# Four products g side by side, TensorE's part of the attention at fewer places, and six buffers for the last x2

## The chip, the cores and the metric

The kernel runs on 1 core of one Trainium2 chip. The metric is the device time of one execution in microseconds (us). TensorE is called PE here, VectorE DVE, ScalarE ACT, GpSimd POOL and SyncE, which issues all DMAs of this kernel, SP.

## The reference, cut to what matters

Three parts follow each other: an attention with 32 memory slots per head over 8 batches of 576 tokens (8 heads of 64), a first feed-forward block (maximum of three products, then an output product) and a second one (a gated product, then an output product).

```python
def _attn_ref(q, k, v, phi):
    a = exp(phi - max(phi, axis=2)); a = a / (sum(a, axis=2) + 1e-09)
    k_m = einsum('bhsm,bhsd->bhmd', a, k)
    v_m = einsum('bhsm,bhsd->bhmd', a, v)
    scores = (1 / sqrt(64)) * q @ k_m.T
    attn = exp(scores - max(scores)); attn = attn / (sum(attn) + 1e-09)
    return attn @ v_m

# x: attention output as 4608 tokens x 512
h = maximum(maximum(x @ w1, x @ w2), x @ w3)        # 4608 x 768
x2 = h @ moe_w_out                                  # 4608 x 512
gate = 1 / (1 + exp(-(x2 @ w_gate)))                # 4608 x 1536
out = gate * (x2 @ w_val) @ moe2_w_out              # 4608 x 512
```

The weights are float64; the kernel turns their bits into float32 itself. Every product is made of three: each operand is held as a high and a low part in fp32r, and high x low, low x high and high x high are summed (PASSES).

## The kernel before, in words

**Passes.** The first feed-forward block runs in four passes `p` (0 to 3) of two batches, "pairs" in the words of the change. A pass has 24 steps of a first stage (`s` from 0 to 23) and 16 steps of a second one (24 to 39). In the first stage `s = 4 j + u`, where `j` (0 to 5) is a block of 128 of the 768 hidden columns.

**g.** `v_m` times the three weights, for one block `j` and one quarter `hp` of the heads (`g_step`, L383): three products over all 128 rows of the array, 384 columns wide, into one PSUM bank. ACT copies out the high part, DVE subtracts and gives the low part. Each step of the first stage makes one g of the block after its own.

**h.** Attention weights times g, for block `j` and half the tokens of the two batches (`h_part`, L402): 36 products per step, each on 64 rows, two batches beside each other in the array. Two steps fill six banks (three weights, two batches). ACT copies the first pair of banks out (`h_copy`), DVE takes the maximum with the second and the third (`h_max`), ACT and POOL split the result into high and low (`h_keep`).

**x2.** A step of the second stage makes `h @ moe_w_out` for 288 tokens and 128 columns (`x2_step`, L441): 18 products over all 128 rows. DVE or ACT copies the bank into a tile x2 (`x2_keep`, L456), and a DMA stores it. Tile x2 has two buffers.

**Attention.** The attention of the next pass (four sets of heads `n`) is woven into the pass in ten stages a0 to a9 and a split (`stages`, L212 to L334), one stage in a step. PE works in a2 (5 transposes), a3 (40 small products on `kv`, in tiles of 32 columns), a4 (2 transposes) and a5 (8 products with `q`, in tiles of 64 columns). Set `n` begins at step `a_at + 8 n`, with `a_at` 5 in pass 0 and 2 later, so that three sets or so stand in the first stage. `load_ahead` (L618) loads `phi`, `kv` and `q` of the next set when stages 1, 3 and 5 of a set are reached.

**Weights.** In pass 0 each weight tile wx is loaded raw, turned into float32 by two ACT and three DVE instructions on tile ca (`w_f32`, L126), split by ACT and POOL one step later, and stored; later passes load the stored tile. `w_next` is called once a step for this. The weights of the second feed-forward block are converted in the passes 1 to 3 (`b_next`, 13, 13 and 22 times), spread over steps 1 to 37 of passes 1 and 2 and over the first stage of pass 3.

**Order.** In the passes each engine works through its instructions in the order in which the program gives them, and so does SP with its DMAs; within a step this order is: what is due first (`h_max` of the third weight, copies of x2), PE's attention, g, h or x2, `h_copy`, the weight splits, the copies of g, those of the attention, `h_keep`, the conversions, `h_max` of the second weight, loads, stores. There are 8 PSUM banks. In the prologue, in the second stage of pass 3 and after it a planner places the instructions by its own estimates. After the passes comes the second feed-forward block (tiles px, pz, pv, po), for which the PSUM banks are handed over (L774 to L777).

```python
            g = None
            if s < NS:
                j, u = divmod(s, 4)
                if j + 1 < J:
                    g = g_step(p, j + 1, u)
                    next(g)
                h_part(p, j, u // 2, u % 2 == 0)
```

Of the kernel before, what the change touches and what calls it, by code (L numbers as in the profile page):

```python
# [18 lines left out]
def attn_moe_kernel(  # L19
# [148 lines left out]
    def load_phi(n):  # L168
        st = A[n] = {"kv": [], "q": []}
        if n in (2, 3):  # L170
            st["phi"] = early(S)
        else:
            st["phi"] = att.tile([128, S], F32, tag="phi", name="phi", bufs=2)
        for b in range(2):
            m, pr = source(n, b)
            dma(st["phi"][64 * b:64 * b + 64], phiT[m, 64 * pr:64 * pr + 64])

    def load_kv(n):
        for c in (0, 2):
            if n < 4:  # L180
                t = early_tile()[:, :1024]
            else:
                t = att.tile([128, 1024], F32, tag="kv", name="kv", bufs=3)
            t = t.rearrange("p (c x) -> p c x", c=2)
            for b in range(2):
                m, pr = source(n, b)
                dma(t[:, :, 256 * b:256 * b + 256],
                    kvm[m, c:c + 2, :, 256 * pr:256 * pr + 256].rearrange("c s x -> s c x"))
            A[n]["kv"] += [t[:, 0], t[:, 1]]
        if n < 4:  # L190
            t = early(512)
        else:
            t = att.tile([128, 512], F32, tag="kvt", name="kvt", bufs=1)
        for b in range(2):
            m, pr = source(n, b)
            dma(t[:64, 256 * b:256 * b + 256], kvt[m, :, 256 * pr:256 * pr + 256])
        A[n]["kv"].append(t)

    def load_q(n, e):
        if (n, e) in ((0, 0), (0, 1)):  # L200
            t = early(S)
        else:
            t = att.tile([128, S], F32, tag="q", name="q", bufs=3)
        m, pr = source(n, e)
        dma(t, qT[m, pr])
        A[n]["q"].append(t)
# [112 lines left out]
    def a9(n):  # L319
        st = A[n]  # L320
        yield
        stg = st["stg"] = att.tile([128, S], F32, tag="stg", name="stg", bufs=4)
        vec.transpose(out=stg, in_=st["s"].rearrange("p a m -> p (a m)"))

    AT = {}
# [128 lines left out]
        return ps  # L454

    def x2_keep(p, u, d, ps):  # L456
        t = low.tile([128, U], F32, tag="x2", name="x2", bufs=2)
        copy(vec if u % 2 == 0 or p == NP - 1 else act, t, ps[:, :U])
        t0 = p * 2 * S + u * U
        return lambda: dma(x2s[:, d, t0:t0 + U], t)  # L460

    def run(*gens):
        gens = list(gens)
        while gens:
            gens = [x for x in gens if next(x, 1) is None]
# [151 lines left out]

    def load_ahead(k, n):  # L618

        if n + 1 < NBG:  # L620
            if k == 1:
                load_phi(n + 1)
            elif k == 3:
                load_kv(n + 1)
            elif k == 5:
                load_q(n + 1, 0)
                load_q(n + 1, 1)
# [5 lines left out]
    for hp in range(4):  # L633
        w_step()
        run(g_step(0, 0, hp))
    bplan = [(j + h * NJ, n) for j in range(NJ) for h in range(2) for n in range(4)]


# [9 lines left out]
    for p in range(NP):  # L648
        last = p == NP - 1
        side, loads, convs = {}, {}, {}  # L650

        def at(pos, fn, *a, where=None):
            where = side if where is None else where
            where.setdefault(min(int(pos), NS + NX - 1), []).append((fn, a))

        if last:
            att.release()
            br = tc.alloc_tile_pool(name="br", bufs=1, side="right", reuse_waits="tile")
            at(NS, x_load, 0)
            at(NS, tw_load, 0)  # L660
            at(NS + 1, x_sums, 0, 0)
            at(NS + 2, x_sums, 0, 1)
            at(NS + 2, t_make, 0, ORDER[0])
            for n, pr in enumerate(ORDER):
                at(NS + 3 + n * 0.8, x_split, 0, pr, vec if n % 2 else None)
                if n:
                    at(NS + 8 + n * 0.8, t_make, 0, pr)
            at(NS + 14, wo_make, 0)

        def w_next():  # L670
            if plan:
                w_want(*plan.pop(0))
            split, store = w_have()
            if split:
                later["splits"].append(split)
            if store:
                later["stores"].append(store)

        def b_next():
            store = b_have()  # L680
            if store:
                later["stores"].append(store)

        for j in range(2, J):
            for hp in range(4):
                at(4 * (j - 2) + hp, w_next, where=convs)
        if p == 0:
            def wo1_begin():
                plan.extend((-1, n, 0) for n in range(J * DM // PC))
                w_fill()  # L690
            at(4 * (J - 2) - 3, wo1_begin, where=loads)
            for n in range(J * DM // PC):
                at((17, 19, 21, 23, 25, 27, 28, 29)[n], w_next, where=convs)
        if not last:
            def w1_begin(p=p):
                plan.extend((j, hp, p + 1) for j in range(J) for hp in range(4))
                w_fill()
            at(28, w1_begin, where=loads)
            for n in range(8):
                at(30 + n, w_next, where=convs)  # L700
        if p:
            def b_start():
                while len(bq) < 2 and bplan:
                    b_want()
            n_b = 22 if last else 13
            end = NS - 1 if last else NS + NX
            at(0, b_start, where=loads)
            for n in range(n_b):
                at(1 + n * (end - 1) / n_b, b_next, where=convs)
        a_at = 2 if p else 5  # L710
        atts = {}
        if not last:
            if p == 0:
                for n, k in enumerate((1, 3, 5)):
                    at(n, load_ahead, k, 3, where=loads)
            for n in range(4):
                for k in range(len(stages)):
                    atts.setdefault(a_at + 8 * n + k, []).append((k, 4 * p + 4 + n))
                at(max(NS + n, a_at + 8 * n + len(stages)), a_split, 4 * p + 4 + n)
        for s in range(NS + NX):  # L720
            if last and s == NS:
                order["kept"] = queue["in order"] = False
                mid.release()
                b1 = tc.alloc_tile_pool(name="b1", bufs=1, side="right", reuse_waits="tile")
            later = {"first": [], "splits": [], "stores": []}
            hold = []
            take("first")
            gens = [stages[k](n) for k, n in sorted(atts.get(s, ()), reverse=True)]
            for x in gens:
                next(x)  # L730
            g = None
            if s < NS:
                j, u = divmod(s, 4)
                if j + 1 < J:
                    g = g_step(p, j + 1, u)
                    next(g)
                h_part(p, j, u // 2, u % 2 == 0)
            else:
                d, u = divmod(s - NS, 4)
                if not last and 32 <= s < 36:  # L740
                    g = g_step(p + 1, 0, s - 32)
                    next(g)
                ps = x2_step(p, u, d)
            if s < NS and u % 2:
                h_copy(j, u // 2)
            take("splits")
            if g:
                next(g, 1)
            for x in gens:
                next(x, 1)  # L750
            take("hold")
            for fn, a in side.get(s, ()):
                fn(*a)
            for fn, a in convs.get(s, ()):
                fn(*a)
            if s < NS and u % 2:
                h_max(j, u // 2, 1)
                later["first"].append(lambda j=j, hf=u // 2: h_max(j, hf, 2))
                hold.append(lambda j=j, hf=u // 2: h_keep(j, hf))
            elif s >= NS:  # L760
                def keep(p=p, u=u, d=d, ps=ps):
                    due["stores"].append(x2_keep(p, u, d, ps))
                later["first"].append(keep)
            for k, n in atts.get(s, ()):
                load_ahead(k, n)
            for fn, a in loads.get(s, ()):
                fn(*a)
            take("stores")
            due.update(later)
            due["hold"] = hold  # L770
# [203 lines left out]
```

## Time and profile before

| | us |
|---|---|
| median of 3 runs | 1428.8 (1425.76 to 1428.92) |
| the profiled execution: its time | 1428.41 |
| the profiled execution: its span | 1426.6 |
| PE busy | 1367.4 (96%) |
| weight loads busy, beside PE | 1184.2 (83%) |
| DVE busy | 818.6 (57%) |
| ACT busy | 514.2 (36%) |
| POOL busy | 485.4 (34%) |

The span is the time from the first to the last instruction. Matmuls are pipelined: a row's own duration overlaps the next row's, so the time that a group of products takes is read from its start to the start of the next row. A bracket at the end of a row is the idle time of that engine before it and what ended it. All tiles of PSUM banks in the passes are called `ps`, so a row is known by what it reads: `ps<-wx,vt` is g, `ps<-attn,g` is h, `ps<-h,wo` is x2, `ps<-ident,et`, `ps<-kv,es`, `ps<-kvt,es`, `ps<-ident,kvb` and `ps<-q,kt` are the attention's a2, a3, a3, a4 and a5.

### The profile page before, as it was taken

The numbers are of one execution on the slowest core, as the hardware profiler recorded it, in microseconds if no ns is written. First come the engines' busy times: TensorE is split into PE (matmuls) and PEld (weight loads), VectorE is DVE, ScalarE is ACT, GpSimd is POOL, SyncE is SP. The second block draws the span as 40 slices with busy tenths as digits, with TensorE's granted clock in tenths as the row PEclk, the third lists the DMA queues.
The fourth block names the chain that finished last, engine by engine and source line by source line (L and its number), as shares of the span: only waits on it lengthen the run. The fifth ranks groups of instructions, "written<-read, shape, count | busy, mean of one in ns | idle before, by whom it ended". The sixth has DMA issues, their size and how long they took to land.

```text
span 1426.6 us, 25129 instructions
## 1 busy us (share of the span) xinstructions
PE 1367.4 (96%) x9592; PEld 1184.2 (83%) x9592; DVE 818.6 (57%) x1425; ACT 514.2 (36%) x1062; POOL 485.4 (34%) x394
## 2 busy tenths in 40 slices
PE   5598999999999999799999999999999999999998
PEld 3377988889889988788888888888888899999997
DVE  4777736755766686666775445554355544454454
ACT  4465524433443453254344222242222322143221
POOL 1544511231222113754478211182112721161211
PEclk8699999999999999899999999999999999999999
DMA  9676567567656975675547644566444666566661
GB/s 276 230 237 223 173 199 234 165 216 244 209 173 205 294 246 160 235 277 192 192 179 264 206 148 148 175 213 203 159 151 158 220 232 230 180 236 225 221 207 71
DMA packets 122008, 292.64 MB, mean 205 GB/s; under 512 B 13088, under 2 KB 47904, under 8 KB 121888
## 3 DMA queue, kind: packets, MB, share of 16 engines
q1 hardware_dynamic: 121888, 291.03, 61.6%
q8 instruction: 76, 1.25, 0.4%
q14 instruction: 44, 0.36, 0.1%
HBM read 224.92 MB, written 66.06 MB: 204 GB/s over the span
## 4 chain that ended last, share of the span: by engine, by line
PE 81%; DVE 8%; DMA 4%; issue 2%; ACT 2%; POOL 2%; SPq 0%; DVEq 0%; ACTq 0%; POOLq 0%
PE ps L61 24%; PE po L61 21%; PE px L61 16%; PE pz L61 10%; PE pv L61 10%; DVE ca L61 4%; DMA early<-kvm_dram 1%; DVE hm L61 1%; DMA raw<-wx_dram 1%; DVE sm L61 1%; ACT g L61 1%; POOL xf L61 1%; DVE g L61 1%; DMA x2s<-x 1%; ACT ca L61 0%
## 5 line engine op out<-in xcount | busy, mean ns | idle before, releaser
L61 PE MATMUL po<-wo,gg 128*128 128x512 f32 x1296 | 327.8, 392 | 1.0 <-POOL gg L61 1.0
L61 POOL TENSOR_TENSOR gg<-gf,gg 128x512 fp32r<-128x512 f32 (+1 forms) x120 | 143.1, 1192 | 474.2 <-ACT gg L61 433.2
L61 PE MATMUL ps<-attn,g 64*128 64x288 f32 x3456 | 263.8, 300 | 21.1 <-DVE hm L61 9.6
L61 PEld LDWEIGHTS po<-wo,gg 128*128 128x128 f32 x1296 | 242.4, 188 | 49.5 <-POOL gg L61 1.3
L61 PEld LDWEIGHTS ps<-attn,g 64*128 64x128 f32 x3456 | 237.9, 186 | 49.0 <-issue 20.3
L61 PE MATMUL px<-xa,tb 128*128 128x512 f32 (+1 forms) x1080 | 245.7, 370 | 9.7 <-DVE x L61 9.7
L61 PEld LDWEIGHTS px<-xa,tb 128*128 128x128 f32 x1080 | 199.5, 189 | 38.2 <-issue 9.9
L61 DVE TENSOR_TENSOR acc<-po,acc 128x512 f32<-128x512 f32 x180 | 124.3, 690 | 175.9 <-PE po L61 174.9
L61 PE MATMUL pv<-xa,tb 128*128 128x512 f32 (+1 forms) x720 | 169.5, 367 | 0.0
L61 PE MATMUL pz<-xa,tb 128*128 128x512 f32 (+1 forms) x720 | 169.1, 367 | 0.0
L61 PE MATMUL ps<-h,wo 128*128 128x288 f32 x1152 | 159.9, 297 | 0.2 <-ACT h L61 0.2
L61 PEld LDWEIGHTS ps<-h,wo 128*128 128x128 f32 x1152 | 155.7, 189 | 2.9 <-issue 1.5
L61 PEld LDWEIGHTS pz<-xa,tb 128*128 128x128 f32 x720 | 132.1, 188 | 18.6
L61 PEld LDWEIGHTS pv<-xa,tb 128*128 128x128 f32 x720 | 131.9, 188 | 17.7
L61 ACT CAST gg<-gf 128x512 fp32r<-128x512 f32 (+1 forms) x120 | 69.4, 578 | 177.9 <-DVE gf L61 173.5
L61 DVE TENSOR_TENSOR u<-pz,p 128x512 f32<-128x512 f32 (+1 forms) x120 | 76.2, 635 | 94.9 <-PE pz L61 90.4
L61 POOL TENSOR_TENSOR h<-hm,h 128x576 fp32r<-128x576 f32 x48 | 68.7, 1432 | 174.1 <-ACT h L61 173.6
L61 ACT ACTIVATE sg<-sg 128x512 f32<-128x512 f32 (+1 forms) x90 | 53.1, 590 | 142.7 <-DVE sg L61 142.6
L61 DVE TENSOR_TENSOR g<-ps,g 128x384 fp32r<-128x384 f32 x96 | 53.1, 553 | 78.7 <-ACT g L61 78.6
L61 POOL TENSOR_TENSOR xa<-xf,xa 128x512 fp32r<-128x512 f32 (+1 forms) x64 | 79.2, 1259 | 22.2 <-ACT xa L61 18.8
L61 DVE TENSOR_TENSOR hm<-ps,hm 128x288 f32<-128x288 f32 x192 | 75.1, 449 | 10.5 <-PE ps L61 10.4
L61 ACT CAST g<-ps 128x384 fp32r<-128x384 f32 x96 | 46.2, 481 | 89.0 <-PE ps L61 88.5
(86 smaller groups left out, 1352.7 us busy)
## 6 DMA issues: line engine op xcount, KB each, us to landing
tb<-tbs SPq DMA_DIRECT2D x168, 512.0 KB, 3.9
wx<-wxs SPq DMA_DIRECT2D x72, 384.0 KB, 4.0
wo<-wos SPq DMA_DIRECT2D x48, 512.0 KB, 5.0
tbs<-tb SPq DMA_DIRECT2D x42, 512.0 KB, 2.9
raw<-wb_dram SPq DMA_DIRECT2D x48, 384.0 KB, 4.4
kv<-kvm_dram SPq DMA_DIRECT2D x48, 256.0 KB, 4.8
raw<-wx_dram SPq DMA_DIRECT2D x24, 384.0 KB, 3.4
wxs<-wx SPq DMA_DIRECT2D x24, 384.0 KB, 3.6
```

The source lines that it names most:

```text
L61: ins = fn(*a, **k)
```

## The change

The four g of a block stand together at the first step of the block before it. The attention's stages get a table of steps (A_AT) by which PE's part stands in steps 16 and 20 or in the second stage. To go with it, the tile wx is asked for one step earlier (the first one of pass 0 in the prologue), `phi` is loaded two sets ahead, `kvt` and `q` get one more buffer and `stg` two fewer. The conversions for the second block in passes 1 and 2 move into the first stage. In pass 3 tile x2 is taken from another pool, with six buffers in place of two.

```diff
@@ load_kv, load_q, a9
-            t = att.tile([128, 512], F32, tag="kvt", name="kvt", bufs=1)
+            t = att.tile([128, 512], F32, tag="kvt", name="kvt", bufs=2)
-            t = att.tile([128, S], F32, tag="q", name="q", bufs=3)
+            t = att.tile([128, S], F32, tag="q", name="q", bufs=4)
-        stg = st["stg"] = att.tile([128, S], F32, tag="stg", name="stg", bufs=4)
+        stg = st["stg"] = att.tile([128, S], F32, tag="stg", name="stg", bufs=2)
@@ x2_keep
-        t = low.tile([128, U], F32, tag="x2", name="x2", bufs=2)
+        if p == NP - 1:
+            t = b1.tile([128, U], F32, tag="x2", name="x2", bufs=6)
+        else:
+            t = low.tile([128, U], F32, tag="x2", name="x2", bufs=2)
@@ load_ahead
+        if k == 1 and n + 2 < NBG:
+            load_phi(n + 2)
         if n + 1 < NBG:
-            if k == 1:
-                load_phi(n + 1)
-            elif k == 3:
+            if k == 3:
@@ before the passes
         run(g_step(0, 0, hp))
+    w_step()
@@ the passes
         for j in range(2, J):
             for hp in range(4):
-                at(4 * (j - 2) + hp, w_next, where=convs)
+                if 4 * (j - 2) + hp or p:
+                    at(max(4 * (j - 2) + hp - 1, 0), w_next, where=convs)
...
-            end = NS - 1 if last else NS + NX
             at(0, b_start, where=loads)
             for n in range(n_b):
-                at(1 + n * (end - 1) / n_b, b_next, where=convs)
-        a_at = 2 if p else 5
+                at(1 + n * (NS - 2) / n_b, b_next, where=convs)
         atts = {}
+        A_AT = (
+            (14, 15, 16, 20, 24, 25, 26, 27, 28, 29, 30),
+            (18, 19, 20, 24, 26, 27, 28, 29, 30, 31, 32),
+            (22, 23, 24, 27, 29, 30, 31, 32, 33, 34, 35),
+            (25, 26, 27, 30, 32, 33, 34, 35, 36, 37, 38),
+        )
         if not last:
             if p == 0:
-                for n, k in enumerate((1, 3, 5)):
-                    at(n, load_ahead, k, 3, where=loads)
+                for n, (k, m) in enumerate(((1, 2), (1, 3), (3, 3), (5, 3))):
+                    at(n, load_ahead, k, m, where=loads)
             for n in range(4):
                 for k in range(len(stages)):
-                    atts.setdefault(a_at + 8 * n + k, []).append((k, 4 * p + 4 + n))
-                at(max(NS + n, a_at + 8 * n + len(stages)), a_split, 4 * p + 4 + n)
+                    atts.setdefault(A_AT[n][k], []).append((k, 4 * p + 4 + n))
+                at(A_AT[n][-1], a_split, 4 * p + 4 + n)
...
-            g = None
+            gs = []
             if s < NS:
                 j, u = divmod(s, 4)
-                if j + 1 < J:
-                    g = g_step(p, j + 1, u)
+                if j + 1 < J and u == 0:
+                    gs = [g_step(p, j + 1, hp) for hp in range(4)]
+                for g in gs:
                     next(g)
                 h_part(p, j, u // 2, u % 2 == 0)
             else:
                 d, u = divmod(s - NS, 4)
                 if not last and 32 <= s < 36:
-                    g = g_step(p + 1, 0, s - 32)
-                    next(g)
+                    gs = [g_step(p + 1, 0, s - 32)]
+                    next(gs[0])
...
-            if g:
-                next(g, 1)
-            for x in gens:
+            for x in gs + gens:
                 next(x, 1)
```

## Rows read from the trace of the kernel before

**Rows 1.** Busy time by stage: stretch, length, PE, PEld, DVE, ACT, POOL, clock, DMA.
```profile
66.35:160.06 93.71, 86.57 (x1043) 74.06 (x1041) 73.38 (x153) 54.82 (x128) 39.60 (x34) 0.95 0.65 211
...
210.64:297.43 86.79, 86.24 (x1087) 73.70 (x1086) 57.87 (x125) 39.24 (x95) 20.48 (x16) 1.00 0.62 200
297.43:342.13 44.70, 44.26 (x357) 42.66 (x356) 25.05 (x48) 15.50 (x35) 11.76 (x9) 1.00 0.75 252
...
474.67:555.53 80.86, 78.41 (x922) 68.22 (x921) 64.43 (x127) 42.08 (x98) 15.71 (x12) 1.00 0.76 235
...
604.12:1426.60 822.48, 817.47 (x3816) 703.85 (x3816) 421.38 (x635) 243.38 (x438) 288.21 (x238) 1.00 0.57 195
```

**Rows 2.** Timeline of PE, first stage of pass 1: start, own duration, work.
```profile
247.51 2.66 PE L61 MATMUL ps<-attn,g 64*128 64x288 f32 x36
250.10 0.79 PE L61 MATMUL ps<-wx,vt 128*128 128x384 f32 x3
250.82 2.67 PE L61 MATMUL ps<-attn,g 64*128 64x288 f32 x36
```

**Rows 3.** Timeline of PE, steps 19 to 22 of pass 0.
```profile
145.33 9.80 PE L61 MATMUL ps<-attn,g 64*128 64x288 f32 x144
155.41 0.77 PE L61 MATMUL ps<-ident,et 128*128 128x128 f32 x5 [0.28 <-ACT et L61]
```

**Rows 4.** Timeline of PE, second stage of pass 1.
```profile
307.68 0.77 PE L61 MATMUL ps<-ident,et 128*128 128x128 f32 x5 [0.44 <-ACT et L61]
...
310.75 1.08 PE L61 MATMUL ps<-kv,es 128*32 128x128 f32 x32
...
320.94 0.69 PE L61 MATMUL ps<-wx,vt 128*128 128x384 f32 x3
321.47 2.54 PE L61 MATMUL ps<-h,wo 128*128 128x288 f32 x18
323.84 0.68 PE L61 MATMUL ps<-wx,vt 128*128 128x384 f32 x3
```

**Rows 5.** Timeline of DVE, first stage of pass 3.
```profile
516.92 1.54 DVE L61 TENSOR_TENSOR hm<-ps,hm 128x288 f32<-128x288 f32 x4
...
519.64 1.25 DVE L61 TENSOR_SCALAR ca<-ca 128x384 uint32<-128x384 uint32 x1 [0.72 <-ACT ca L61]
...
524.13 1.54 DVE L61 TENSOR_TENSOR hm<-ps,hm 128x288 f32<-128x288 f32 x4
...
546.13 1.54 DVE L61 TENSOR_TENSOR hm<-ps,hm 128x288 f32<-128x288 f32 x4
...
552.87 1.54 DVE L61 TENSOR_TENSOR hm<-ps,hm 128x288 f32<-128x288 f32 x4
```

**Rows 6.** Timeline of DVE, steps 2 to 5 of pass 0.
```profile
74.96 0.56 DVE L61 SCALAR_TENSOR_TENSOR ca<-raw,ca 128x384 uint32<-128x384 uint32 x1
...
83.36 0.56 DVE L61 SCALAR_TENSOR_TENSOR ca<-raw,ca 128x384 uint32<-128x384 uint32 x1
84.87 0.56 DVE L61 TENSOR_TENSOR g<-ps,g 128x384 fp32r<-128x384 f32 x1 [0.96 <-ACT g L61]
```

**Rows 7.** Timeline of PE, pass 0: the longest stall of the first stage.
```profile
125.46 1.06 PE L61 MATMUL ps<-attn,g 64*128 64x288 f32 x11 [3.63 <-DVE hm L61]
```

**Rows 8.** Timeline of DVE, end of pass 3.
```profile
595.54 1.53 DVE L61 TENSOR_TENSOR wo<-tw,wo 128x512 fp32r<-128x512 f32 x1 [1.51 <-ACT wo L61]
...
603.51 0.46 DVE L61 COPY x<-ps 128x288 f32<-128x288 f32 x1 [3.87 <-DMA x2s<-x]
```

**Rows 9.** Timeline of PE, start of the second feed-forward block.
```profile
604.12 4.75 PE L61 MATMUL px<-xa,tb 128*128 128x512 f32 x12 [9.66 <-DVE x L61]
608.71 2.88 PE L61 MATMUL pz<-xa,tb 128*128 128x512 f32 x12
```

**Rows 10.** Timeline of SP, second stage of pass 1: start, time to issue.
```profile
313.22 1.85 SPq L70 DMA_DIRECT2D kvt<-kvt_dram  x2
```

**Rows 11.** DMA issues from 284 to 345 us: count, size, median us to landing.
```profile
kvt<-kvt_dram SPq DMA_DIRECT2D x4, 64.0 KB, 4.5
```

## The prediction

> **What bounds the kernel now.** I read the stretches by stage first, then PE's timeline inside a stage, then what releases PE where it stands still. The stages show PE nearly full everywhere: 86.24 of 86.79 us in the first stage of pass 1, 44.26 of 44.70 in its second, and 817.47 of 822.48 in the second feed-forward block [rows 1]. Two stretches are looser: the first stage of pass 0 (7.1 us of PE idle in 93.7) and that of pass 3 (2.4 in 80.9). A third hole is one single wait, 9.66 us between the last x2 product and the first px [rows 9]. So a gain must come from fewer PE nanoseconds per product or from these three places.
>
> PE's timeline gives the first of these. In a step of pass 1 the three products of g take 250.82 - 250.10 = 0.72 us, the 36 of h 250.10 - 247.51 = 2.59 [rows 2]. The same three between x2 products, all on full rows, take 321.47 - 320.94 = 0.53 [rows 4]; and where four steps of h follow each other without g, 144 products take 155.41 - 0.28 - 145.33 = 9.80, or 10.08 with the idle, which I use as 2.52 a step [rows 3]. A visit of g among the h products therefore costs about 0.72 - 0.53 + 2.59 - 2.52 = 0.26 us beyond its own work.
>
> **The change part by part.** The sum is made against the profiled execution, 1428.41 us, of which the span is 1426.6; the median of the runs is 0.4 above it.
>
> *Four g together, passes 1 and 2.* A block costs PE 4 x 0.72 + 4 x 2.59 = 13.24 now. After: 0.72 for the first g, 3 x 0.53 for the others, 10.08 + 0.06 for h, in all 12.45. Five blocks a pass have a g: 5 x 0.79 = 3.95 us, on PE, which bounds the stage. The four evictions are hidden by the next h: ACT and DVE have the whole block for them, and a g is read a block later. In banks, a block takes 4 + 12 = 16, twice through the eight; the first g's need the two banks left over and those that ACT's `h_copy` frees one step earlier. The wx load that used to wait for a g of its own step now waits in SP's queue for the first g of the next block, at every fourth step, by at most a step (2.5 us); behind it stand raw loads that are used two steps later, and the stores of ca. I cost that at 0; it would show as DVE or ACT waiting for `raw`.
>
> The Trainium skill (TensorE: Matmul & The Clock Gate, Part 3: Packing small matmuls) says that a weight load overlaps running products only if it goes to other rows of the array. By that rule the full-row products of g would pay for their loads however they stand, 12 x 0.24 = 2.88 us a block as now, and this term would be 0. The trace does not bear it out: 0.53 for three beside other full-row products [rows 4].
>
> *The attention's PE work.* A set beside the g's of the first stage costs PE (86.79 - 20 x 3.31 - 4 x 2.59) / 3 = 3.4 us, stalls included [rows 1, 2]. In the second stage four pieces and four x2 steps take 320.94 - 307.68 = 13.26; an x2 step alone 323.84 - 321.47 = 2.37 [rows 4]; so a set costs 3.8 there. Somewhat over two sets a pass move: about 1.0 us more a pass. Bounds: 0 (the steps of x2 ahead of the pieces are slower than 2.37 as well, so that the pieces may be innocent) and 2.5.
>
> The skill's page TensorEngine Tiling (Array Packing), Tiling Modes, says that each change of tiling mode drains the array. By it, with 0.26 us for a change there and back as beside h, nine more pieces a pass between x2 products would cost 2.3 us in place of 1.0. The trace's difference between the two places, 3.8 - 3.4 = 0.4 us for four pieces, is 0.1 a piece [rows 1, 2, 4].
>
> Vector work of the attention leaves the first stage and five conversions a pass enter it (passes 1 and 2). I take DVE's load there as unchanged, 58 us, now in about 75 instead of 86.8: 77%, below the 80% (64.43 of 80.86) at which pass 3 stalls [rows 1]. Passes 1 and 2 together: 2 x (3.95 - 1.0) = 5.9 us.
>
> *Pass 3, first stage.* Here a conversion stands in every step, and DVE sets the pace: the four `hm` recur every 524.13 - 516.92 = 7.21 us, against 6.62 of PE work in two steps; part of it is a wait of 0.72 for ACT. Without any g two steps still take 552.87 - 546.13 = 6.74 [rows 5]. A block after the change is one pair without g (6.74) and one with four DVE subtractions (about 0.46 each from start to start), which partly fill the wait for ACT: 6.74 + 6.74 + 1.84 less 0.7 to 1.9 = 13.4 to 14.6, against 14.42. Taken: 14.1, 5 x 0.3 = 1.5 us. Bounds: -4.5 (no wait filled) and 4 (PE bounds again).
>
> *Pass 0, first stage.* Two steps take 83.36 - 74.96 = 8.40 us on DVE, which also waits for ACT behind the weight split (0.96) [rows 6]. Four g's in one step lengthen a block by up to 0.5 (the same subtractions, but the waits at the other three steps stay, since ACT's split stands ahead of them): three blocks, -1.5. The attention leaves the steps 5 to 13, and with it the stalls behind `hm`, such as 3.63 us [rows 7]. PE's 7.1 us of idle [rows 1] is what that can return; the two sets moved cost 1.0 in the second stage. 7.1 - 1.5 - 1.0 = 4.6 us. A g for hp 3 now uses a split made one step before; late DVE work makes PE wait there, but in these blocks PE waits for DVE anyway. The extra conversion in the prologue has PE's wait for the first attention weights as its cover. Bounds: -1.5 and 11 (all blocks PE-bound).
>
> *Six buffers for x2.* The last x2 product ends at 604.12 - 9.66 = 594.46 [rows 9]; the last copies wait for the stores that free the two buffers, the last of them 3.87 us, and it ends at 603.97 [rows 8]. With six, the three copies behind the wo subtraction come at 597.07 + 3 x 0.46 = 598.4 at the latest if the order stays (5.7 us earlier), or right behind the products, near 595.0 (9.1). The first 12 products then took 4.59 us against 2.7 for the next 12 [rows 9]: after the long idle they ran for a time at the lower clock (1.2 GHz in place of 2.4); up to 1.9 comes back. Next in line are the tw loads, needed 38 us later. Taken: 8.0. Bounds: 2 (in this stretch the planner orders anew, and may put other DVE work ahead of the copies) and 11. The tile now lies where an earlier pool lay; a wait for that could hold the first copy 2 us, but banks are free then.
>
> Sum: 5.9 + 1.5 + 4.6 + 8.0 = 20.0 us; 1428.41 - 20.0 = 1408.4, as a median 1408.5 to 1409. I forecast 1408.5.
>
> **The rivals.**
> - *DVE bounds all first stages.* Shorter steps with 13 conversions in passes 1 and 2 may fall into pass 3's pattern. Then their 5.9 and the 1.5 are gone, and half of pass 0's gain: 1428.4 - 10.3 = 1418. For: 77% against 80%. Against: about one conversion in two steps, not two.
> - *The weight loads of g are paid wherever it stands.* Then grouping returns nothing on PE: passes 1 and 2 lose 1.0 each by the moved attention, pass 3 gains nothing, and 1428.4 - 8.0 - 4.6 + 2.0 = 1418. The rule of the skill's page on weight loads above says this; against it stand the 0.53 us [rows 4].
> - *The end of pass 3 hardly closes* because the planner sets the copies late: 2 in place of 8, 1414.5. For: its order is open there. Against: it knows that six buffers are free.
> - *Pass 0 gains more*, since without attention PE leads: 11 in place of 4.6, with 9 to 10 at the end of pass 3: 1400.
> - *Slower: `kv` comes late in the second stage.* Half of a set's `kv` can only be asked for when the a3 before it has run. In pass 1 that a3 began at 310.75 [rows 4], the last `kvt` load was issued by 315.07 [rows 10] and such loads land 4.5 us later [rows 11]: 8.9 us. The new table puts a3 three steps apart, 10.5 us with their pieces, and `q` is queued ahead of `kv`. If the crowd stretches 8.9 to some 14.5, each of two a3 a pass stalls 4 us and PE restarts at the lower clock, 1.5 us more: 3 x 2 x 5.5 = 33 us, 1428 - 20 + 33 = 1441. It decides from 3.4 us a stall. Against: the slack of 1.6 us, and that the conversions' traffic leaves this stage.
>
> **How the numbers follow.** Forecast 0.47 (its own range 1403 to 1414); DVE 0.16; paid weight loads 0.02; the late end 0.13; more in pass 0 0.15; slower 0.07. A difference under 0.3% (4.3 us) can't be told from none: 0.03 of the DVE case and 0.01 each of the late end and the slower case fall there. Faster 0.89, same 0.05, slower 0.06. Range 1396 to 1420: above lie the slower case and the tail of the DVE case, below the best of pass 0.
>
> **What would show it.** Twelve products on wx in one row of 2.3 us and 144 on attn of 10.1 behind it; first stages of passes 1 and 2 of about 75.5 us and second ones of 52 to 53; pass 3's first stage of 79; the wait before px under 5 us. Wrong it would be if PE's waits for `hm` or for loads in steps 20 to 33 come to more than 5 us a pass, or if the twelve products take 2.9.

## The result, and the profile after

The changed kernel took 1412.3 us (median of 4 runs, 1409.8 to 1418.1) beside 1428.2 for the kernel before: a ratio of 0.9897 [0.9864, 0.9931]. The profiled execution is the longest of the four, 1418.07 us with a span of 1416.3. It gains 10.3 us on the profiled one of before; the same kernel profiled once more (experiment 1) gains 20.3 on it, with a span of 1406.3.

Busy time by stage of the kernel after (columns as in [rows 1]): the first and second stage of passes 0, 1 and 2 in turn and the first of pass 3, each from the last product of the stage before; then the second feed-forward block.

```profile
63.00:157.40 94.40, 82.05 (x962) 76.43 (x964) 67.20 (x133) 53.32 (x122) 36.53 (x32) 0.88 0.61 202
157.40:217.40 60.00, 54.85 (x476) 49.30 (x473) 34.43 (x71) 20.84 (x51) 21.66 (x18) 0.94 0.73 225
217.40:292.50 75.10, 73.73 (x976) 70.21 (x975) 54.18 (x116) 40.19 (x92) 15.79 (x11) 1.00 0.66 214
292.50:350.30 57.80, 54.76 (x472) 49.26 (x471) 24.28 (x55) 15.00 (x38) 16.40 (x13) 0.94 0.69 220
350.30:423.10 72.80, 72.68 (x976) 69.82 (x975) 54.89 (x116) 40.18 (x92) 15.76 (x11) 1.00 0.67 216
423.10:475.00 51.90, 51.90 (x475) 47.19 (x472) 24.38 (x55) 15.19 (x38) 16.38 (x13) 1.00 0.63 200
475.00:552.30 77.30, 72.28 (x926) 68.76 (x925) 62.13 (x127) 43.41 (x98) 15.84 (x12) 1.00 0.78 251
...
591.30:1416.30 825.00, 816.17 (x3818) 702.13 (x3816) 426.94 (x640) 243.94 (x440) 291.88 (x241) 1.00 0.58 198
```

Read line 6 against line 4. They hold the same work, that of the second stage with the moved attention; in pass 2 PE is busy for all of its 51.90 us, in pass 1 it stands still for 3.04 of 57.80 and the mean clock is 0.94. With the stages cut in the same way in the trace of before, a pass 1 or 2 took 87.3 and then 44.8 or 44.6 us. Read more finely, from the first g that stands behind the x2 products of one pass to the first behind those of the next, pass 2 went from 474.06 - 342.13 = 131.93 us to 475.09 - 350.48 = 124.61 and gained 7.3; pass 1 went from 132.10 to 132.98 and lost 0.9.

Timeline of PE after, first stage of pass 1 (start, own duration, work), which answers to [rows 2]:

```profile
255.81 2.36 PE L61 MATMUL ps<-wx,vt 128*128 128x384 f32 x12
258.10 9.80 PE L61 MATMUL ps<-attn,g 64*128 64x288 f32 x144
267.83 0.77 PE L61 MATMUL ps<-ident,et 128*128 128x128 f32 x5
```

Twelve g in 258.10 - 255.81 = 2.29 us and 144 products of h in 267.83 - 258.10 = 9.73: a block takes 12.02 in place of 13.24. The twelve weight loads of the g are busy for 2.04 of the 2.29 us.

Where pass 1 lost it: the same trace, second stage of pass 1, first PE, then ACT, then SP's queue.

```profile
322.48 2.53 PE L61 MATMUL ps<-h,wo 128*128 128x288 f32 x18
328.05 2.19 PE L61 MATMUL ps<-q,kt 128*64 128x288 f32 x8 [3.04 <-ACT kt L61]
330.17 1.33 PE L61 MATMUL ps<-wx,vt 128*128 128x384 f32 x3
331.29 3.96 PE L61 MATMUL ps<-h,wo 128*128 128x288 f32 x18
```

```profile
326.48 0.40 ACT L61 COPY x<-ps 128x288 f32<-128x288 f32 x1 [8.15 <-DMA x2s<-x]
326.77 0.48 ACT L61 CAST g<-ps 128x384 fp32r<-128x384 f32 x1
327.14 0.70 ACT L61 ACTIVATE s<-s 128x576 f32<-128x576 f32 x1
327.73 0.27 ACT L61 COPY kt<-ps 128x128 f32<-128x128 f32 x1
```

```profile
316.53 0.91 SPq L70 DMA_DIRECT2D q<-qT_dram  x2
317.53 1.91 SPq L70 DMA_DIRECT2D kv<-kvm_dram  x4
319.49 1.11 SPq L70 DMA_DIRECT2D kvt<-kvt_dram  x2
320.70 0.53 SPq L70 DMA_DIRECT2D x2s<-x  x1
```

PE waits for the copy kt. On ACT this copy stands behind a copy of x2 that waited 8.15 us for one of the two x2 buffers; the buffer comes free with a store; and the store that is issued at 320.70 stands in SP's queue behind eight loads of `q`, `kv` and `kvt`. After the wait PE is slow: `q` takes 2.12 us from start to start in place of 1.12 (297.48 to 298.60, earlier in the stage). The granted clock by stretch, PE of the kernel after (length, PE busy, clock, DMA):

```profile
327.60:334.40 6.80, 6.35 (x24) 0.50 0.72 249
334.40:346.00 11.60, 11.60 (x87) 1.00 0.51 154
```

So 3.04 us of waiting are followed by 6.8 us at 1.2 GHz: the stage costs 5.9 us more than that of pass 2. Pass 0 has the same stall at 195.18 (3.38 us, behind an x2 copy of ACT that waited 7.51 us for its store).

PE after, first stage of pass 0 and the start of the second block:

```profile
95.58 0.44 PE L61 MATMUL ps<-wx,vt 128*128 128x384 f32 x1 [0.74 <-ACT wx L61]
...
98.59 11.67 PE L61 MATMUL ps<-attn,g 64*128 64x288 f32 x144 [1.25 <-DVE hm L61]
...
115.80 11.61 PE L61 MATMUL ps<-attn,g 64*128 64x288 f32 x144 [1.25 <-DVE hm L61]
130.77 1.33 PE L61 MATMUL ps<-ident,et 128*128 128x128 f32 x5 [3.36 <-ACT et L61]
131.75 4.19 PE L61 MATMUL ps<-wx,vt 128*128 128x384 f32 x12
...
591.27 1.55 PE L61 MATMUL px<-xa,tb 128*128 128x512 f32 x6
595.28 1.65 PE L61 MATMUL px<-xa,tb 128*128 128x512 f32 x6 [2.46 <-DVE x L61]
```

### The profile page after: what moved, and what is told of

Same layout as the page of the kernel before. It is cut to its first block, busy times and chain, and to the rows that moved or that the text cites. A ratio compares the mean times of both kernels' runs of the same rounds, so it can differ in the third digit from the quotient of the medians.

```text
span 1416.3 us, 25127 instructions
## 1 busy us (share of the span) xinstructions
PE 1352.5 (95%) x9592; PEld 1191.0 (84%) x9592; DVE 814.8 (58%) x1425; ACT 515.1 (36%) x1062; POOL 485.4 (34%) x394
## 3 DMA queue, kind: packets, MB, share of 16 engines
q8 instruction: 76, 1.25, 0.4%
## 4 chain that ended last, share of the span: by engine, by line
PE 82%; DVE 7%; DMA 5%; issue 2%; ACT 1%; SPq 1%; POOL 1%; DVEq 0%; ACTq 0%; POOLq 0%
PE ps L61 26%; PE po L61 21%; PE px L61 15%; PE pv L61 10%; PE pz L61 10%; DVE ca L61 3%; DMA x2s<-x 1%; SPq L70 1%; DMA early<-kvm_dram 1%; DMA q<-qT_dram 1%; DVE hm L61 1%; ACT ca L61 1%; DVE td L61 0%; DVE sm L61 0%; DMA raw<-wb_dram 0%
## 5 line engine op out<-in xcount | busy, mean ns | idle before, releaser
L61 PE MATMUL ps<-attn,g 64*128 64x288 f32 x3456 | 246.4, 298 | 10.3 <-DVE hm L61 10.0
L61 DVE TENSOR_SCALAR ca<-ca 128x384 uint32<-128x384 uint32 x80 | 57.9, 724 | 56.6 <-ACT ca L61 56.6
L61 PE MATMUL ps<-wx,vt 128*128 128x384 f32 x288 | 67.6, 374 | 15.8 <-ACT wx L61 8.7
```

Source lines behind the costliest of these rows:

```text
L61: ins = fn(*a, **k)
```

## The experiments

Theory X: passes 0 and 1 lose 6 us each because the x2 copy on ACT, waiting for its store, holds the attention's kt copy behind it. Its rivals blame the loads themselves (`kv` late), the conversions in the first stage, or say that the moved attention is dear in any case. Theories C and D are on passes 0 and 3. Medians are given; the kernel before stood at 1427.8 to 1428.1 beside them.

**1. The changed kernel again.** No edit.

> The changed kernel once more, unchanged. Its first profile showed PE waiting for ACT's copy kt ahead of a5 in the second stages of pass 0 (1.76 and 3.38 us) and pass 1 (3.04 us), but not of pass 2, which has the same program. Theory X (ACT's copy of x2 waits for a store that lands behind the attention's loads, kt stands behind it on ACT): the waits depend on how transfers interleave, so they change from one execution to the next; second stage of pass 1 anywhere between 51.8 and 57.8 us, time 1409 to 1418, median near 1412. Rival Y (the waits come from the order of the program): the same two waits of 3 us at the same places, second stage of pass 1 again 57.8 us, time near 1418 in the profiled execution.

1411.4 us, 0.9878 [0.9864, 0.9892]. First and second stages of passes 0 to 2: 152.3 (here from the start of the span) and 58.9, 73.5 and 55.5, 72.8 and 51.8. PE's wait for kt in pass 1 came at the same place, but 2.05 us long in place of 3.04: it changes from one execution to the next, as theory X said. The expectation was wrong in one point: pass 2 does not have the same program, since there is no further set of heads whose `q`, `kv` and `kvt` would crowd SP's queue; two loads of `q` stand there (443.81) in place of the eight. That fits theory X, for pass 2 has no stall.

**2. A buffer of its own for the x2 that DVE copies**, passes 0 to 2, so that ACT's has two.

```diff
+        elif u % 2 == 0:
+            t = att.tile([128, U], F32, tag="x2e", name="x2e", bufs=1)
         else:
             t = low.tile([128, U], F32, tag="x2", name="x2", bufs=2)
```

> The changed kernel, but in passes 0 to 2 ACT's copies of x2 have the two buffers to themselves and DVE's get one of their own, so that a copy of ACT waits for a store four steps back in place of two. Theory X: the waits of PE for kt behind x2 copies go; second stages of passes 0 and 1 near 53 and 52 us (59.8 and 57.8 in the first profile), time 1405 to 1409. Rival Y (kt is late for ACT's weight splits, or the loads of kv and q are late): the waits stay, time 1410 to 1414.

1401.7 us, 0.9815 [0.9802, 0.9829]; second stage of pass 1 51.9, of pass 0 53.6.

**3. A step's stores issued ahead of its loads**, with two buffers as before.

```diff
+            take("stores")
             for k, n in atts.get(s, ()):
                 load_ahead(k, n)
...
-            take("stores")
```

> The changed kernel, but at the end of each step the stores are asked for ahead of the loads in SP's queue. Theory X: the store that ACT's copy of x2 waits for no longer lands behind 12 loads of kv, kvt and q; waits for kt in the second stages under 1 us, time 1405 to 1409. Rival Z (the loads themselves are the tight resource): now kv or q land later, and PE waits for them at a3 or a5 instead; time 1410 to 1416.

1401.1 us, 0.981 [0.9796, 0.9823]; second stages 53.6, 51.9, 51.9. ACT in pass 1, the same place:

```profile
312.23 0.40 ACT L61 COPY x<-ps 128x288 f32<-128x288 f32 x1 [3.83 <-PE ps L61]
...
313.89 0.26 ACT L61 COPY kt<-ps 128x128 f32<-128x128 f32 x1
```

The x2 copy waits for PE's products, no longer for a store. Two different edits, each on one link of the chain, return the same 10 us: theory X is shown. The loads of `q` and `kv` are all still there, so a late `kv` is not the cause. What stays in pass 0, a wait of 1.8 us for kt, has another cause (the split of `wo` that stands ahead of kt on ACT waits 3.65 us for DVE).

**4. Control: the kernel before, with the diff of experiment 3 alone.**

> The kernel before with one edit: a step's stores are issued ahead of its loads. If the stall behind the x2 copy belongs to the moved attention, there is none here to take away: second stages of passes 1 and 2 stay at 44.8 and 44.6 us, the time at 1428 (within 2). If the store order gains by itself whatever the attention does, the time falls by 4 us or more, to 1424 or less, and the 10 us of the same edit on the changed kernel are not all the move's.

1427.6 us, 0.9994 [0.9986, 1.0003]. The stall belongs to the moved attention.

**5. Attention where it was**, with the buffers that `kvt`, `q` and `stg` had before; the rest of the change kept.

```diff
-                    atts.setdefault(A_AT[n][k], []).append((k, 4 * p + 4 + n))
+                    atts.setdefault(a_at + 8 * n + k, []).append((k, 4 * p + 4 + n))
```

> The changed kernel with the attention where it was (steps a_at + 8 n, with the buffers of before for kvt, q and stg); g grouped, six buffers in pass 3 and the conversions as in the change. The prediction's terms: pass 0 loses most of what the moved attention returned there (the stalls behind hm come back, some 5 us), passes 1 and 2 gain 1 us each: 1415. Theory X: the second stages go back to 44.7 us, since PE's attention work beside g cost little and its loads are spread again, and the first stages of passes 1 and 2 are near 82 us (87.4 before): passes 1 and 2 gain 5 us each, pass 3 and its end 11, pass 0 about 0: 1407. If moving the attention was what helped, 1418 or more.

1411.3 us, 0.988 [0.9867, 0.9894], between the 1415 of the prediction's terms and the 1407 of theory X. Pass 2 of this run, first and second stage (PE busy, clock, DMA):

```profile
337.90:422.70 84.80, 83.16 (x1091) 1.00 0.69 229
422.70:466.80 44.10, 44.10 (x358) 1.00 0.54 173
```

Grouping alone takes pass 2 from 131.9 to 128.9 us, and moving the attention takes it on to 124.6: the move gains 4.3 where it doesn't stall. Of this, 2.7 us are PE time (127.26 busy against 124.58); the rest are waits, above all 1.4 us for hm in the first stage of this run, of which the kernel after has none in pass 2. The moved pieces cost 51.9 - 44.1 = 7.8 us in the second stage and 84.8 - 72.8 = 12.0 in the first, waits included. PE in the first stage of pass 2 shows why:

```profile
352.65 2.64 PE L61 MATMUL ps<-attn,g 64*128 64x288 f32 x36
355.22 1.08 PE L61 MATMUL ps<-kv,es 128*32 128x128 f32 x32
...
356.58 2.64 PE L61 MATMUL ps<-attn,g 64*128 64x288 f32 x36
359.15 0.44 PE L61 MATMUL ps<-ident,kvb 128*128 128x128 f32 x2
359.52 2.67 PE L61 MATMUL ps<-attn,g 64*128 64x288 f32 x36
362.11 1.19 PE L61 MATMUL ps<-q,kt 128*64 128x288 f32 x8
```

A step of h takes 2.57 to 2.59 us from start to start, as it did beside g [rows 2], against 9.73 / 4 = 2.43 undisturbed. Wherever an attention piece stands among the h, the block is cut up again, and grouping the g's returns less: 3.0 us of the 7.3. No run moves the attention alone in a pass that PE bounds.

**6. Only the six buffers, on the kernel before.**

```diff
+        if p == NP - 1:
+            t = b1.tile([128, U], F32, tag="x2", name="x2", bufs=6)
```

> The kernel before with one thing of the change, six buffers for x2 in pass 3. The prediction gives this term 8.0 us (2 to 11): 1420. By the traces of before and after the wait ahead of px falls by 9.7 us, and some 2.7 of it come back later, where DVE stands waiting for tw and PE for u: 7 us, 1421. Rival (the end of pass 3 was closed by the new order of the planner, not by the buffers): under 3 us, 1425 or more.

1422.2 us, 0.9952 [0.9939, 0.9965]: 5.9 us less in medians, as the wait ahead of px falls from 9.66 to 3.66.

**7. Two buffers again, in the kernel of experiment 3.**

```diff
-            t = b1.tile([128, U], F32, tag="x2", name="x2", bufs=6)
+            t = b1.tile([128, U], F32, tag="x2", name="x2", bufs=2)
```

> The changed kernel with stores ahead of loads, and x2 of pass 3 with two buffers again. If the six buffers are worth the same here as alone on the kernel before (6.0 us), the time is 1407 and px waits about 9 us again for the last x2 copy. Rival: stores ahead of loads already free the buffers sooner (in this stretch the planner sets the order), and the loss is under 3 us, 1404 or less.

1404.9 us, 0.9833 [0.982, 0.9846]: 3.8 us over experiment 3, between the two expectations. Here px starts at once in spite of two buffers, and waits in its middle, for the x copies of the second bank:

```profile
572.15 1.55 PE L61 MATMUL px<-xa,tb 128*128 128x512 f32 x6
580.15 2.93 PE L61 MATMUL px<-xa,tb 128*128 128x512 f32 x6 [6.46 <-DVE x L61]
```

So part of what the end of pass 3 gained is not the buffers'. The other runs show whose it is. With the attention where it was (experiment 5: g grouped, six buffers) px waits ahead of its first product as it does with the buffers alone:

```profile
586.48 5.36 PE L61 MATMUL px<-xa,tb 128*128 128x512 f32 x12 [3.79 <-DVE x L61]
```

With the stores ahead alone (experiment 4) it waits 9.90 us. Of the runs with the moved attention, none waits there. So the move, with the buffers that go with it, lets px start at once; by what way is open.

**8. Pass 0: weights asked for two steps earlier** (on the kernel of experiment 3; two tiles in the prologue).

```diff
-                if 4 * (j - 2) + hp or p:
-                    at(max(4 * (j - 2) + hp - 1, 0), w_next, where=convs)
+                i = 4 * (j - 2) + hp
+                if p:
+                    at(max(i - 1, 0), w_next, where=convs)
+                elif i > 1:
+                    at(i - 2, w_next, where=convs)
```

> The kernel with the stores ahead of the loads (1401.1), and in pass 0 the conversion of wx one more step earlier (two more weight tiles in the prologue in place of one). In pass 0 PE waits 3.5 us for wx ahead of the grouped g, and 3.4 us at the lower clock follow each of three such waits. Theory C (the steps of pass 0 go at the pace of the chain DVE, ACT, weight split, 17.2 us a block, and PE's wait for wx is only where the slack shows): the waits for wx go, others behind hm take their place, first stage of pass 0 within 1 us, time 1400 to 1402. Rival W (the waits for wx and the low clock behind them cost their time): pass 0 gains 4 to 8 us, time 1393 to 1397.

1399.7 us, 0.9796 [0.9784, 0.9809]. PE in pass 0:

```profile
98.25 11.70 PE L61 MATMUL ps<-attn,g 64*128 64x288 f32 x144 [3.20 <-DVE hm L61]
...
115.47 11.71 PE L61 MATMUL ps<-attn,g 64*128 64x288 f32 x144 [3.20 <-DVE hm L61]
127.47 0.77 PE L61 MATMUL ps<-ident,et 128*128 128x128 f32 x5 [0.29 <-ACT et L61]
```

The waits for wx are gone and waits for hm stand in their place, 9.96 us in all. A block takes 115.47 - 98.25 = 17.22 us, as after the change (115.80 - 98.59 = 17.21). From its first h to its last the stage took 88.8 us (90.9 in experiment 3), and the median fell by 1.4: a little more than theory C allowed, and far from the 4 to 8 us of rival W. Theory C holds for the period: DVE and ACT set the pace of pass 0, wherever PE is made to wait for it.

**9. Pass 0: one g per step again** (on the kernel of experiment 3).

```diff
+                if j + 1 < J and p == 0:
+                    gs = [g_step(p, j + 1, u)]
-                if j + 1 < J and u == 0:
+                elif j + 1 < J and u == 0:
```

> The kernel with the stores ahead of the loads (1401.1), but in pass 0 one g a step as before. Theory C (pass 0 goes at the pace of the chain, and grouping neither helps nor hurts there): first stage of pass 0 within 2 us, time 1399 to 1403. Rival V (four evictions in one step lengthen the chain, 0.5 us a block in the prediction, and the waits for wx come on top): pass 0 shorter by 3 to 6 us, time 1395 to 1398. Rival U (grouping returns 0.8 us a block in pass 0 too): slower, 1404 or more.

1400.3 us, 0.9801 [0.9789, 0.9814]: 0.9 less than experiment 3, within the intervals. Grouping in pass 0 neither gains nor costs what can be measured. In PE's timeline the products that wait for hm come every two steps, at 84.77 and 93.16, 8.39 us apart as DVE's work was before [rows 6], and the granted clock is 1.00 from 66 to 93 us. So the pace is nearly the same (16.8 us a block against 17.2) with PE at its upper level, and the lower level at which the 144 products of experiment 8 take 11.7 us is not what sets it.

**10. Conversions 17, 17 and 14 in passes 1 to 3, in place of 13, 13 and 22** (on the kernel of experiment 3).

```diff
-            n_b = 22 if last else 13
+            n_b = 14 if last else 17
```

> The kernel with the stores ahead of the loads (1401.1), but the 48 conversions for the second block shared as 17, 17 and 14 over the passes 1 to 3 in place of 13, 13 and 22. Theory D (in pass 3 conversions in every step make DVE the bound of the first stage, while passes 1 and 2 have room): the waits for hm in pass 3 fall from 5.0 us to under 1.5, those of passes 1 and 2 rise by 1 us at most in all; first stage of pass 3 near 73.5 us (77.3), time 1396 to 1398. Rival (the burst of four g evictions makes the waits for hm): they stay above 3.5 us in pass 3 and rise by 2 us or more in each of passes 1 and 2; time 1400 to 1404.

1396.3 us, 0.977 [0.9753, 0.9787]. Pass 3's first stage falls from 77.3 to 69.5 us and its 5.0 us of waits for hm to none; passes 1 and 2 pay 4.5 and 1.5. Theory D holds for pass 3: DVE, with a conversion in nearly every step, was the bound. It was wrong about the room in passes 1 and 2, which it let pay 1 us in all, and that the time fell into its range is luck: 3.7 us came from the end, where it had nothing (820.4 us from the last x2 product to the end of the span, 824.0 in experiment 3).

**11. Conversions of passes 1 and 2 spread over the whole pass again** (on the kernel of experiment 3).

```diff
-                at(1 + n * (NS - 2) / n_b, b_next, where=convs)
+                at(1 + n * ((NS - 1 if last else NS + NX) - 1) / n_b, b_next, where=convs)
```

> The changed kernel with stores ahead of loads, and the conversions of passes 1 and 2 spread over the whole pass again as before. Theory: with four g together the first stages of these passes are bound by PE (72.7 us in pass 2 with the conversions in it), so taking 5 of 13 conversions out returns at most 0.5 us each; in the second stage they stand in ACT's and DVE's queues ahead of the attention's and the x2 copies, and their loads beside kv: 1 to 4 us more in each, in all 1403 to 1408 against 1401.1. Rival: the cover is enough in either place, within 1.5 us of 1401.

1401.6 us, 0.9811 [0.9797, 0.9824]. Pass 1: 72.3 and 53.5 us (73.7 and 51.9 in experiment 3), pass 2: 72.3 and 51.8. The rival was right: with the stores ahead, it does not matter in which stage they stand.

**12. What these runs pointed to, in one**: experiments 2, 3, 8 and 10, with the conversions of pass 1 from step 4.

```diff
-                at(1 + n * (NS - 2) / n_b, b_next, where=convs)
+                b0 = 4 if p == 1 else 1
+                at(b0 + n * (NS - 1 - b0) / n_b, b_next, where=convs)
```

> All that the runs pointed to in one: stores ahead of loads, a buffer of their own for the x2 that DVE copies, conversions 17, 17 and 14 in passes 1 to 3 (in pass 1 from step 4), weights of pass 0 asked for two steps earlier. Theory: the gains lie in different stages and add: 1396.3 less 1.4 (weights) less 3 (pass 1's first stage back from 78.2 to about 75), some 1392. Rival: pass 0 and pass 1 go at the pace of ACT and DVE whatever the order, and it stays at 1395 to 1397.

1392.4 us, 0.9746 [0.9733, 0.9759], the fastest; against experiment 10 the intervals overlap. The sum came out as expected, its terms did not. Pass 1's first stage grew to 80.0 us (78.2 in experiment 10) instead of falling to 75, because with 17 conversions in fewer steps DVE, and no longer PE, sets the pace:

```profile
242.58 2.38 PE L61 MATMUL ps<-wx,vt 128*128 128x384 f32 x12
247.28 10.16 PE L61 MATMUL ps<-attn,g 64*128 64x288 f32 x144 [2.33 <-DVE hm L61]
```

Pass 0 gave more than was asked of it, 205.2 us to its last product against 208.3.

## Why the prediction was right, and where its terms were wrong

1412.3 lies in the forecast's own range and 3.8 us over the value. Yet the sum was helped by errors that cancelled. Terms against the profiled executions of before and after, in us gained:

| term | predicted | measured |
|---|---|---|
| pass 1 (g together, attention moved) | 2.95 | -0.9 (6.6 in experiment 3) |
| pass 2 (the same) | 2.95 | 7.3 |
| pass 3, first stage | 1.5 | 4.1 |
| pass 0 (measured from the start of the span) | 4.6 | -7.5 |
| end of pass 3 to the end | 8.0 | 7.2 (9.7 ahead of px, 2.5 given back) |
| sum, with 0.1 in pass 3's second stage | 20.0 | 10.3 |

The profiled execution is the longest of its four. By the profile of experiment 1, the shortest of its four, the gains are 3.1 in pass 1, 7.3 in pass 2, 4.3 in pass 3, -1.4 in pass 0 and 7.0 at the end, in all 20.3. That this is the sum of the forecast is luck: passes 2 and 3 gave 7 us more than their terms, and pass 0 gave 6 less.

*Four g together.* The mechanism was right: twelve in 2.29 us (2.31 predicted). The step of h was mis-sized: 10.14 a block predicted, 9.73 measured. The row it came from [rows 3] gives 9.80 without the 0.28 us for which PE waits for et behind it; the prediction counted this wait as work of PE. The Trainium skill (TensorE: Matmul & The Clock Gate, Part 3: Packing small matmuls) says that a weight load overlaps running products only on other rows of the array. Here twelve full-row products take 0.19 us each, their weight loads are busy for 2.04 of these 2.29 us, and the rule does not hold for them.

*The attention's PE work* is the step with the wrong sign: -1.0 a pass predicted, +4.3 in pass 2 (experiment 5), of which 2.7 are PE time. The prediction priced a set among the h at 3.4 us from a stage where nearly every step had a g as well [rows 1, 2]: an attention piece beside a g shared its visit. With the g's gone it keeps the whole price of cutting into the h. The two edits don't add: grouping alone returned 3.0 us in pass 2, and both together 7.3 where the prediction had 2.95. What the move would return without grouping no run shows.

*Waits in the second stage.* The slower rival looked at the right crowd, `q` and `kv` in SP's queue, but at the wrong victim. It asked when `kv` lands; what came late was a store of x2 queued behind them, and through it ACT, kt and PE. That copies of x2 wait for stores, the prediction had seen at the end of pass 3; of the stores in passes 0 to 2 it named only those of ca, in the first stage. It set 3.4 us a stall as the point from which that case decides; 3.04 and 3.38 came in the profiled execution, two in all where the rival had six, with 2.9 us of lower clock behind the one in pass 1 (5.9 - 3.04). Experiments 2 and 3 put the price at 10 us.

*Pass 0* failed as a term. "Four g's in one step lengthen a block by up to 0.5" was right: 17.21 against 2 x 8.40 [rows 6]. "What that can return" was wrong. In experiment 9, where g stands as before, the first stage takes 151.85 - 61.87 = 90.0 us from the g of step 1 to the end of its h, against 158.69 - 66.35 = 92.3 before, and the second stage 53.6 against 51.3: taking the attention out of steps 5 to 13 returned 2.4 us of the 7.1 and cost 2.3, since DVE and ACT set the pace there (experiments 8 and 9). The stall of 3.63 [rows 7] is gone, and one of 3.36 for et stands near its place. ACT makes et after a weight split that waits 1.56 us for DVE. In ACT's timeline after:

```profile
129.43 0.51 ACT L61 CAST wx<-ca 128x384 fp32r<-128x384 f32 x1 [1.56 <-DVE ca L61]
129.85 0.77 ACT L61 ACTIVATE et<-phi,nm 128x576 f32<-128x576 f32 x1
```

The second stage's kt stalls did the rest: 60.0 us against 53.6 in experiment 3. How long the prologue lasts differs between executions (the first h of pass 0 starts at 61.7 us in experiment 1 and at 65.6 in the profiled execution after); that is part of the -7.5, and no run shows it to be the change's.

*Pass 3, first stage.* The mechanism held, DVE bounds it; the size was 4.1 us, just past its upper bound of 4. DVE after, at the four hm, to set against [rows 5]:

```profile
502.36 1.54 DVE L61 TENSOR_TENSOR hm<-ps,hm 128x288 f32<-128x288 f32 x4
503.82 1.94 DVE L61 TENSOR_TENSOR g<-ps,g 128x384 fp32r<-128x384 f32 x4
...
509.11 1.54 DVE L61 TENSOR_TENSOR hm<-ps,hm 128x288 f32<-128x288 f32 x4
...
511.84 1.25 DVE L61 TENSOR_SCALAR ca<-ca 128x384 uint32<-128x384 uint32 x1 [1.19 <-ACT ca L61]
...
515.85 1.54 DVE L61 TENSOR_TENSOR hm<-ps,hm 128x288 f32<-128x288 f32 x4
```

With four g's the two steps take 509.11 - 502.36 = 6.75, without any 6.74. The four subtractions stand where DVE would have waited for ACT's ca, and fill that wait whole; the prediction let them fill 0.7 to 1.9 of a block.

*Six buffers.* Predicted 8.0; 5.9 alone (experiment 6), 3.8 on top of the rest (experiment 7). The wait ahead of px closed by 9.7, and two waits took its place: 2.46 for x of the second bank (above) and 1.66 for u. "Next in line are the tw loads, needed 38 us later" was wrong about DVE: the subtraction on tw stands in DVE's order ahead of what PE needs now.

```profile
599.76 0.69 DVE L61 TENSOR_TENSOR u<-pz,p 128x512 f32<-128x512 f32 x1 [0.67 <-PE pz L61]
604.79 1.25 DVE L61 TENSOR_TENSOR td<-tw 128x512 f32<-128x512 f32 x1 [4.34 <-DMA tw<-wbf]
```

The next u stands behind four such instructions, and PE waits for it (1.66). The lower clock at the first px [rows 9] is gone, as predicted, which is why only 2.5 of the 4.1 us are seen: the first twelve px take 1.55 + 1.49 us beside the wait, against 4.59. In experiments 10 and 12, with fewer conversions in pass 3, the wait for x is gone; it is gone in experiment 9 as well, with 22 of them, so their number alone does not explain it.

*The rivals.* "DVE bounds all first stages" fell: passes 1 and 2 took 75.1 and 72.8 us, with 1.2 us and no wait for hm; at 17 conversions it begins to come true (experiments 10 and 12). "Paid weight loads" and "the end hardly closes" fell; "pass 0 gains more" did too. The marks set for the trace were met, but for the second stages of passes 0 and 1 and the first stages of passes 2 and 3 (72.8 and 77.3, not 75.5 and 79). PE's waits in steps 20 to 33 came to 1.76 + 3.38 = 5.1 us in pass 0, past the 5 us at which the prediction called itself wrong, but for kt and not for hm or a load.

Open is how the moved attention lets px start earlier (experiment 7), and how much of pass 0's gain in experiment 12 is its own.

## What to carry to other kernels

Ask of a moved step not only whether its data arrive, but what else stands in the queue that it lengthens: here a store behind loads, then a copy behind the store, then PE behind the copy. Two edits that take away visits to the same stretch of products must be priced together, since the price of a visit falls only when the last visitor is gone (here 3.0 us a pass for the first, and 2.7 of PE time more for the second). Where an engine already sets the pace, taking a wait out elsewhere only renames it: read the period, not the wait.

## What the runs showed of the hardware

Short waits of PE in pass 0 are followed by the lower clock too: in each block waits such as the 0.74 us for wx and the 1.25 us for hm stand ahead of the h, and the 144 products from 115.80 to 130.77 - 3.36 take 11.6 us in place of 9.73, at a mean clock of 0.85. The wait of 3.36 for et is followed by twelve g in 4.12 us in place of 2.29.

What a wait of PE costs beyond its length differed. In pass 1, 3.04 us of waiting cost 5.9, and 2.05 us cost 3.7 (experiment 1: 55.5 against 51.8). The 1.76 us that stay in pass 0 cost no more than themselves (experiment 3: 53.6 against 51.9), and the q behind them take 1.12 us, as at full speed. Where DVE sets the pace, the lower clock cost little: a block of pass 0 takes 17.2 us with it and 16.8 without (experiments 8 and 9).

Weight loads were hidden beside products on the same rows: twelve loads and twelve products on all 128 rows, 384 columns wide, together took 2.29 us, and the loads were busy for 2.04 of them.
